# Early stage of an attention and gated-MLP kernel: VectorE takes all differences, one per head for q and k together, from operands in four blocks of columns

## The chip, the cores and the metric

The kernel runs on one core of a Trainium2 chip. Its engines work side by side, each through a queue of its own, in order: TensorE (PE in the profile) multiplies matrices, VectorE (DVE), ScalarE (ACT) and GpSimd (POOL) work element by element, and SyncE (SP) issues the DMAs. The metric is the time of one execution on the device in microseconds.

## The reference

Block-causal attention over 8 batches of 8 heads, 576 positions and a head size of 64, followed by a gated MLP over the 4608 tokens:

```python
scores = scale * q @ k.T                    # scale = 1/8
scores = where(block_i >= block_j, scores, -1e9)     # blocks of 64 positions
attn = exp(scores - max(scores)); attn = attn / (attn.sum() + 1e-9)
x = (attn @ v) with the heads side by side           # 4608 x 512
a = x @ w1; b = x @ w2                               # 512 x 1024 each
out = (a * b @ w3) @ w_out                           # 1024 x 1024, then 1024 x 512
```

## The kernel before

**Halves of a number.** Operands of the fast matmul form (fp32r) are kept as a high part, which is the number rounded by a cast, and a low part, the number minus the high part. A product then takes several passes. Every low part is thus a *difference*: a cast writes the high part, and a subtraction of two SBUF operands writes the low part. That subtraction is what the change is about.

**Pairs of heads.** Two heads share the 128 partitions: head j = 0 owns partitions 0 to 63, head j = 1 owns 64 to 127 (`own[j]`, the other half is `oth[j]`). There are 32 pairs, n = 0 to 31. The first four pairs, one batch, are called early (`EARLY = NPAIR`, that is 4). `load(n)` brings q, k and v of a pair into a tile `raw`, of which there are two.

**Scores in two passes.** For each head there are two tiles `hi[j]` and `lo[j]` of 128 x 2 x 576: block 0 belongs to q, block 1 to k. `s_tile` (L224) multiplies block 1 with block 0 of `hi[j]`, then of `lo[j]`, into one sum. In `hi[j]` the own half holds the high parts of q and k, the other half a copy of q's high part and k's low part. In `lo[j]` the own half holds q's low part and a copy of k's high part; the other half holds constants for the block mask and one row with the negated maximum of each query's block, which `shift` (L194) fills by DMA. `prep_qk` (L198) makes all of this in three steps: a cast of q and k together (L203, ScalarE for pairs 1 to 4, VectorE otherwise); two copies between tiles by DMA (L205, L206) and k's low part on GpSimd (L207); q's low part on GpSimd (L209). The two tiles per head have no second buffer.

**The mask's maxima.** `shift_mask` (L161) multiplies coarse bf16 copies of q and k block by block; VectorE reduces each product to its maximum (L183), joins two of the columns (L185), and PE transposes the result.

**The early stage.** Beside the attention of pairs 0 to 3 it prepares the weights: they arrive as 64-bit numbers, and `load_w` (L122) puts each chunk of 128 x 512 together with one instruction of ScalarE (L135) and four of VectorE (L136, L137, L138, L141). There are 40 chunks. 16 of them, of w1 and w2, go on through `load_split` (L145): a cast on ScalarE and a difference on GpSimd (L148). The rest feed the product of w3 and w_out (L360), whose own difference is VectorE's (L349). At the end of a pair `norm` (L321) divides by the sums (GpSimd for pairs 0 and 1, L325), and `finish_x` (L327) makes the high part of x on ScalarE and the low part on GpSimd (L335).

**The late stage.** From about 176 us PE alternates between the attention of pairs 4 to 31 and the MLP (`gen_moe`, L372) of batches already done. `pl` (L250, VectorE) and `gl` (L392, GpSimd) are differences there too, and GpSimd adds up the exponentials (L253).

**Order.** The order in which instructions are written comes from two strings per pair, `EARLY_PLAN` and `PLAN`: "B" takes the next step of `prep_qk` for the pair's second head, "A" for the next pair's first head, "M" the mask, "S" a score tile, "V" the product with v, "C" a step of the weights, "F" one of the MLP, "N", "R", "T" the end of a head or a pair, "Q" v and the next load. Each of the two plans has three "A" and three "B". A planner then places instructions on each engine by its own costs; the attention of early pairs goes ahead of the weights (`high_priority`); in the late stage the order on PE is the written one (`manual_schedule`).

Of the kernel before, what the change touches and what calls it, by code (L numbers as in the profile page):

```python
# [7 lines left out]
F32 = mybir.dt.float32  # L8
F32R = mybir.dt.float32r
# [49 lines left out]
def block_causal_attention__then__gated_mlp_kernel(ctx, tc, qkv, consts, ident_in, w1, w2, w3t, wout, out_t):  # L59
# [18 lines left out]

    hi = [cpool.tile([P, 2, S], F32R, name=f"hi{j}") for j in range(2)]
    lo = [cpool.tile([P, 2, S], F32R, name=f"lo{j}") for j in range(2)]
    w2h = cpool.tile([P, NC, DF], F32R, name="w2h")
    w2l = cpool.tile([P, NC, DF], F32R, name="w2l")

# [13 lines left out]
    cst = raws.tile([P, RAW], F32, tag="raw", name="cst")  # L99
    nc.sync.dma_start(out=cst[0:D, 0 : 2 * S], in_=consts)  # L100
    for j in range(2):
        nc.vector.tensor_copy(lo[j][oth[j]], cst[0:D, 0 : 2 * S].rearrange("p (t s) -> p t s", t=2))
    nc.gpsimd.memset(qd, 0.0)

    tl = {}
# [39 lines left out]
    def load_split(dst_h, dst_l, src):  # L145
        val = load_w(None, src.unsqueeze(1), 1)
        nc.scalar.copy(dst_h, val)
        nc.gpsimd.tensor_tensor(out=dst_l, in0=val, in1=dst_h, op=ALU.subtract)  # L148

    def load_rows(dst_h, dst_l, src, c):  # L150
        for h in range(2):
# [4 lines left out]
    def cast(n, dst, src, act):  # L156
        (nc.scalar.copy if 0 < n <= EARLY or act else nc.vector.tensor_copy)(dst, src)  # L157
# [3 lines left out]
    def shift_mask(n):  # L161
        r = raw_of[n]
        rqk = r[:, 0 : 2 * S].rearrange("p (t s) -> p t s", t=2)
        kb = work.tile([P, S], BF16, tag="kb", name=f"kb{n}")
        cast(n, kb, rqk[:, 1, :], CAST[1])
        for j in range(2):
            cast(n, qd[own[j], :, own[j]], rqk[own[j], 0, :].rearrange("p (i r) -> p i r", r=BLK), CAST[2])
        yield
        m = work.tile([P, 32], F32, tag="m", name=f"m{n}")

        groups = [((7, 0, 512),), ((8, 0, 512),), ((6, 0, 448), (0, 0, 64)), ((5, 0, 384), (1, 0, 128)),
                  ((4, 0, 320), (2, 0, 192)), ((3, 0, 256), (8, 512, 576))]
        for g, parts in enumerate(groups):
            t = ps_q.tile([P, 512], F32, tag="psq", name=f"mx{n}_{g}")
            at = 0
            done = []
            for i, a, b in parts:
                sc = t[:, at : at + b - a]
                nc.tensor.matmul(sc, qd[:, i, :], kb[:, a:b], start=True, stop=True)  # L179
                done.append((sc, 9 if a else i))  # L180
                at += b - a
            for sc, col in done:
                nc.vector.reduce_max(m[:, col : col + 1], sc, axis=AX.X)  # L183
            yield
        nc.vector.tensor_tensor(out=m[:, 8:9], in0=m[:, 8:9], in1=m[:, 9:10], op=ALU.max)  # L185
        mt = ps_q.tile([P, 512], F32, tag="psq", name=f"mt{n}")
        nc.tensor.transpose(out=mt[0:NB, 0:P], in_=m[:, 0:NB], identity=ident)
        ms = work.tile([16, P], F32R, tag="ms", name=f"ms{n}")
        nc.scalar.mul(out=ms[0:NB], in_=mt[0:NB, 0:P], mul=-1.0)
        ms_of[n] = ms  # L190
        shift(n, 0)
        yield

    def shift(n, j):  # L194
        row = lo[j][oth[j].start : oth[j].start + 1, 0, :].rearrange("p (i r) -> p i r", r=BLK)
        nc.sync.dma_start(out=row.bitcast(F32), in_=ms_of[n][0:NB, j * BLK : (j + 1) * BLK].bitcast(F32))

    def prep_qk(n, j):  # L198
        rqk = raw_of[n][:, 0 : 2 * S].rearrange("p (t s) -> p t s", t=2)
        o, x = own[j], oth[j]  # L200
        if j == 1:
            shift(n, 1)
        cast(n, hi[j][o], rqk[o], CAST[0])  # L203
        yield
        nc.sync.dma_start(out=hi[j][x, 0, :].bitcast(F32), in_=hi[j][o, 0, :].bitcast(F32))  # L205
        nc.sync.dma_start(out=lo[j][o, 1, :].bitcast(F32), in_=hi[j][o, 1, :].bitcast(F32))  # L206
        nc.gpsimd.tensor_tensor(out=hi[j][x, 1, :], in0=rqk[o, 1, :], in1=hi[j][o, 1, :], op=ALU.subtract)  # L207
        yield
        nc.gpsimd.tensor_tensor(out=lo[j][o, 0, :], in0=rqk[o, 0, :], in1=hi[j][o, 0, :], op=ALU.subtract)  # L209
        yield  # L210

    def prep_v(n, j):
# [11 lines left out]
    def s_tile(n, j, parts, p_early):  # L224
# [3 lines left out]
        for c, q0, q1, e0 in parts:  # L228
            kr = slice(c * P, min((c + 1) * P, S))
            ks = slice(0, kr.stop - kr.start)  # L230
            for s, src in enumerate((hi[j], lo[j])):
                nc.tensor.matmul(t[ks, at : at + q1 - q0], src[:, 1, kr], src[:, 0, q0:q1], start=(s == 0), stop=(s == 1))  # L232
            todo.append((c, ks, at + e0 - q0, e0, q1))
            at += q1 - q0
        for c, ks, at, q0, q1 in todo:
# [85 lines left out]
    def norm(n, x32, rr):  # L321
        nc.vector.reciprocal(rr, rr)
        rb = work.tile([P, S], F32, tag="tr", name=f"rb{n}")
        nc.vector.transpose(rb, rr.unsqueeze(2).broadcast_to([P, S // 32, 32]))
        (nc.gpsimd if n < 2 else nc.vector).tensor_tensor(out=x32, in0=x32, in1=rb, op=ALU.mult)  # L325

    def finish_x(n, x32):  # L327
        for h in range(2):
# [3 lines left out]
            xl = pool.tile([P, HALF], F32R, tag="xl", name=f"xl{n}_{h}", bufs=bufs)  # L332
            src = x32[:, h * HALF : (h + 1) * HALF]
            nc.scalar.copy(xh, src)
            nc.gpsimd.tensor_tensor(out=xl, in0=src, in1=xh, op=ALU.subtract)  # L335
            x_of[n // NPAIR, n % NPAIR, h] = (xh, xl)

    def gen_w(wp):
# [200 lines left out]
```

## Time and profile before

| | |
|---|---|
| median of 3 runs | 1026.23 us (1025.86 to 1026.67) |
| profiled execution, its own time | 1025.84 us |
| span of its instructions | 1024.1 us |
| mean granted TensorE clock | 0.98 |
| VectorE busy, whole span | 754.3 us (74%) |
| GpSimd busy, whole span | 599.1 us (58%) |

The page names an instruction group by line, engine, operation and tiles, output first: `hi<-raw,hi` writes `hi` from `raw` and `hi`. Behind the count stand the busy time in us, the mean duration of one in ns, the idle time of the engine ahead of these instructions and what ended it. A row of the stages gives the window, its length, the busy us of each engine with counts, then the granted clock of PE, the share of the DMA engines and GB/s.

### The profile page before, as it was taken

What the parts mean: (1) busy time and instruction counts of PE and PEld (TensorE: products, weight loads), DVE (VectorE), ACT (ScalarE), POOL (GpSimd) and SP (SyncE); (2) the same over time, 40 slices, a digit from 0 to 9 for tenths busy, and PEclk for the clock granted to TensorE, in tenths of its full rate; (3) what the DMA queues carried; (4) which work ended last, traced back from release to release, by engine and by line L of the source; (5) the groups of instructions that cost most, each with busy time, mean ns of one, the idle gap of its engine ahead of it and who ended that gap; (6) DMA issues with size and microseconds to landing.
All of it is one profiled execution on the core that took longest, in us unless ns stands there. A gap on an engine that the chain in (4) does not pass through costs nothing.

```text
span 1024.1 us, 18507 instructions
## 1 busy us (share of the span) xinstructions
PE 966.5 (94%) x6624; PEld 886.8 (87%) x6624; DVE 754.3 (74%) x1320; ACT 547.3 (53%) x1433; POOL 599.1 (58%) x625
## 2 busy tenths in 40 slices
PE   4789686999999999999999999999999999999998
PEld 2435344999999999999999999999999999999998
DVE  6999996787778777778777877777777777775100
ACT  4545455655565555556555556555555556554221
POOL 3334365766666676757575767666676757673211
PEclk9899898999999999999999999999999999999999
DMA  7765542221222222222222212221222221110000
GB/s 230 227 212 158 191 128 60 61 69 44 67 72 66 66 66 78 60 83 59 74 60 84 56 49 62 71 73 54 79 60 83 60 84 49 48 25 25 1 25 24
DMA packets 37437, 80.42 MB, mean 79 GB/s; under 512 B 5409, under 2 KB 21921, under 8 KB 37345
## 3 DMA queue, kind: packets, MB, share of 16 engines
q1 hardware_dynamic: 37344, 79.24, 25.7%
q8 instruction: 52, 0.85, 0.4%
q14 instruction: 41, 0.33, 0.1%
HBM read 50.76 MB, written 9.44 MB: 59 GB/s over the span
## 4 chain that ended last, share of the span: by engine, by line
PE 69%; DVE 18%; ACT 6%; issue 4%; DMA 1%; POOL 1%; DVEq 0%; SPq 0%; ACTq 0%; POOLq 0%
PE ab L383 29%; PE o L399 20%; PE s L232 7%; PE x L287 6%; DVE pl L250 5%; PE mx L179 3%; DVE wbits L138 2%; DVE wbits L136 2%; ACT p L247 2%; ACT ph L248 2%; DVE g L390 1%; PE w L360 1%; DVE m L183 1%; DVE wbits L137 1%; PE x L271 1%
## 5 line engine op out<-in xcount | busy, mean ns | idle before, releaser
L253 POOL TENSOR_TENSOR rsum<-rsum,p 128x448 f32<-128x448 f32 x224 | 175.9, 785 | 107.1 <-ACT p L247 100.5
L250 DVE TENSOR_TENSOR pl<-p,ph 128x448 fp32r<-128x448 f32 x168 | 148.9, 900 | 60.7 <-ACT ph L248 59.9
L392 POOL TENSOR_TENSOR gl<-g,gh 128x288 fp32r<-128x288 f32 x128 | 107.5, 840 | 120.4 <-ACT gh L391 119.0
L391 ACT CAST gh<-g 128x288 fp32r<-128x288 f32 x128 | 55.5, 433 | 217.1 <-DVE g L390 217.1
L383 PE MATMUL ab<-xh,w2h 128*128 128x288 f32 x512 | 153.6, 300 | 0.0
L399 PE MATMUL o<-gh,wh 128*128 128x288 f32 x512 | 153.4, 300 | 0.0
L383 PE MATMUL ab<-xl,w1h 128*128 128x288 f32 x512 | 151.0, 295 | 1.3 <-POOL xl L335 1.3
L383 PE MATMUL ab<-xh,w1h 128*128 128x288 f32 x512 | 151.1, 295 | 0.0
L383 PE MATMUL ab<-xl,w2h 128*128 128x288 f32 x512 | 150.9, 295 | 0.0
L383 PE MATMUL ab<-xh,w1l 128*128 128x288 f32 x512 | 150.9, 295 | 0.0
L399 PE MATMUL o<-gl,wh 128*128 128x288 f32 x512 | 150.8, 295 | 0.0
L399 PE MATMUL o<-gh,wl 128*128 128x288 f32 x512 | 150.8, 295 | 0.0
L383 PE MATMUL ab<-xh,w2l 128*128 128x288 f32 x512 | 150.8, 295 | 0.0
L183 DVE TENSOR_REDUCE m<-mx 128x1 f32<-128x512 f32 (+6 forms) x320 | 128.8, 449 | 23.8 <-PE mx L179 22.0
L248 ACT ACTIVATE ph<-s 128x288 fp32r<-128x288 f32 x336 | 131.5, 393 | 0.0
L232 PE MATMUL s<-hi 128*128 128x288 f32 (+4 forms) x384 | 123.8, 334 | 6.3 <-ACT pe L240 4.8
L207 POOL TENSOR_TENSOR hi<-raw,hi 64x576 fp32r<-64x576 f32 x64 | 92.5, 1446 | 37.1 <-ACT hi L157 25.1
L247 ACT ACTIVATE p<-s 128x448 f32<-128x448 f32 x224 | 85.5, 381 | 44.9 <-PE s L232 44.9
L250 DVE TENSOR_TENSOR pl<-rsum,ph 128x288 fp32r<-128x288 f32 x112 | 74.8, 687 | 46.4 <-ACT ph L248 46.3
L390 DVE TENSOR_TENSOR g<-ab,a 128x288 f32<-128x288 f32 x128 | 57.7, 451 | 69.6 <-PE ab L383 61.3
L232 PE MATMUL s<-lo 128*128 128x288 f32 (+4 forms) x384 | 106.4, 306 | 2.1 <-DMA lo<-ms 2.1
L209 POOL TENSOR_TENSOR lo<-raw,hi 64x576 fp32r<-64x576 f32 x64 | 95.6, 1494 | 19.7 <-ACT hi L157 15.0
(73 smaller groups left out, 2449.1 us busy)
## 6 DMA issues: line engine op xcount, KB each, us to landing
raw<-in_qkv SPq DMA_DIRECT2D x32, 896.0 KB
hi<-hi SPq DMA_DIRECT2D x64, 144.0 KB
lo<-hi SPq DMA_DIRECT2D x64, 144.0 KB
out_t<-o SPq DMA_DIRECT2D x64, 144.0 KB
wraw<-in_w3t SPq DMA_DIRECT2D x16, 512.0 KB
wraw<-in_w SPq DMA_DIRECT2D x16, 512.0 KB
wraw<-in_wout SPq DMA_DIRECT2D x8, 512.0 KB
lo<-ms SPq DMA_DIRECT2D x64, 2.2 KB
```

Of the source, the lines that this page charges most:

```text
L183: nc.vector.reduce_max(m[:, col : col + 1], sc, axis=AX.X)
L207: nc.gpsimd.tensor_tensor(out=hi[j][x, 1, :], in0=rqk[o, 1, :], in1=hi[j][o, 1, :], op=ALU.subtract)
L209: nc.gpsimd.tensor_tensor(out=lo[j][o, 0, :], in0=rqk[o, 0, :], in1=hi[j][o, 0, :], op=ALU.subtract)
L232: nc.tensor.matmul(t[ks, at : at + q1 - q0], src[:, 1, kr], src[:, 0, q0:q1], start=(s == 0), stop=(s == 1))
L247: nc.scalar.activation(p32, t[ks, at : at + w], AF.Exp, scale=SCALE)
L248: nc.scalar.activation(ph[ks, o : o + w], t[ks, at : at + w], AF.Exp, scale=SCALE)
L250: nc.vector.tensor_tensor(out=low, in0=p32, in1=ph[ks, o : o + w], op=ALU.subtract)
L253: nc.gpsimd.tensor_tensor(out=r, in0=r, in1=p32, op=ALU.add)
L383: nc.tensor.matmul(t[:, 0:HALF], l[:, c, fs], r, start=(c == 0 and s == 0), stop=(c == NC - 1 and s == 2))
L390: nc.vector.tensor_tensor(out=g32, in0=acc[1][:, 0:HALF], in1=a32, op=ALU.mult)
L392: nc.gpsimd.tensor_tensor(out=gl[:, f, :], in0=g32, in1=gh[:, f, :], op=ALU.subtract)
L399: nc.tensor.matmul(t[:, 0:HALF], l[:, f, es], r[:, f, :], start=(f == 0 and s == 0), stop=(f == NF - 1 and s == 2))
```

## The change

- One tile `qk[j]` of 128 x 4 x 576 takes the place of `hi[j]` and `lo[j]`. Blocks 0 and 1 are q's for the two passes, blocks 2 and 3 are k's. In the own half the cast writes blocks 0 and 3 (`0::3`), the high parts of q and k; one subtraction writes blocks 1 and 2 (`1:3`), the low parts. One DMA copies the high parts to blocks 0 and 2 of the other half (`0::2`), whose blocks 1 and 3 hold the constants. The first pass now multiplies q's high part with k's low part (own half) and with k's high part (other half), the second q's low part with k's high part and the mask.
- `prep_qk` has two steps in place of three. Its one subtraction is VectorE's for pairs 0 to 4, GpSimd's later.
- The differences of the weights, of early x, and the product in `norm` for pairs 0 and 1 move from GpSimd to VectorE.
- The maximum of two columns becomes a reduction over two columns, for all pairs.

```diff
-    hi = [cpool.tile([P, 2, S], F32R, name=f"hi{j}") for j in range(2)]
-    lo = [cpool.tile([P, 2, S], F32R, name=f"lo{j}") for j in range(2)]
+    qk = [cpool.tile([P, 4, S], F32R, name=f"qk{j}") for j in range(2)]
...
-        nc.vector.tensor_copy(lo[j][oth[j]], cst[0:D, 0 : 2 * S].rearrange("p (t s) -> p t s", t=2))
+        nc.vector.tensor_copy(qk[j][oth[j], 1::2, :], cst[0:D, 0 : 2 * S].rearrange("p (t s) -> p t s", t=2))
...
         nc.scalar.copy(dst_h, val)
-        nc.gpsimd.tensor_tensor(out=dst_l, in0=val, in1=dst_h, op=ALU.subtract)
+        nc.vector.tensor_tensor(out=dst_l, in0=val, in1=dst_h, op=ALU.subtract)
...
-        nc.vector.tensor_tensor(out=m[:, 8:9], in0=m[:, 8:9], in1=m[:, 9:10], op=ALU.max)
+        nc.vector.reduce_max(m[:, 8:9], m[:, 8:10], axis=AX.X)
...
-        row = lo[j][oth[j].start : oth[j].start + 1, 0, :].rearrange("p (i r) -> p i r", r=BLK)
+        row = qk[j][oth[j].start : oth[j].start + 1, 1, :].rearrange("p (i r) -> p i r", r=BLK)
...
-        cast(n, hi[j][o], rqk[o], CAST[0])
+        high, low = qk[j][o, 0::3, :], qk[j][o, 1:3, :]
+        cast(n, high, rqk[o], CAST[0])
         yield
-        nc.sync.dma_start(out=hi[j][x, 0, :].bitcast(F32), in_=hi[j][o, 0, :].bitcast(F32))
-        nc.sync.dma_start(out=lo[j][o, 1, :].bitcast(F32), in_=hi[j][o, 1, :].bitcast(F32))
-        nc.gpsimd.tensor_tensor(out=hi[j][x, 1, :], in0=rqk[o, 1, :], in1=hi[j][o, 1, :], op=ALU.subtract)
-        yield
-        nc.gpsimd.tensor_tensor(out=lo[j][o, 0, :], in0=rqk[o, 0, :], in1=hi[j][o, 0, :], op=ALU.subtract)
+        nc.sync.dma_start(out=qk[j][x, 0::2, :].bitcast(F32), in_=high.bitcast(F32))
+        (nc.vector if n <= EARLY else nc.gpsimd).tensor_tensor(out=low, in0=rqk[o], in1=high, op=ALU.subtract)
         yield
...
-            for s, src in enumerate((hi[j], lo[j])):
-                nc.tensor.matmul(t[ks, at : at + q1 - q0], src[:, 1, kr], src[:, 0, q0:q1], start=(s == 0), stop=(s == 1))
+            for s in range(2):
+                nc.tensor.matmul(t[ks, at : at + q1 - q0], qk[j][:, 2 + s, kr], qk[j][:, s, q0:q1], start=(s == 0), stop=(s == 1))
...
-        (nc.gpsimd if n < 2 else nc.vector).tensor_tensor(out=x32, in0=x32, in1=rb, op=ALU.mult)
+        nc.vector.tensor_tensor(out=x32, in0=x32, in1=rb, op=ALU.mult)
...
-            nc.gpsimd.tensor_tensor(out=xl, in0=src, in1=xh, op=ALU.subtract)
+            (nc.vector if n < EARLY else nc.gpsimd).tensor_tensor(out=xl, in0=src, in1=xh, op=ALU.subtract)
```

## The prediction

> **What bounds the kernel now.** I read the page first, then the busy time by stage, then VectorE's waits in the early stage, then its groups of instructions with shapes kept apart, and last the order of time on VectorE and GpSimd side by side.
>
> ```profile
> span 1024.1 us, 18507 instructions
> PE 966.5 (94%) x6624; PEld 886.8 (87%) x6624; DVE 754.3 (74%) x1320; ACT 547.3 (53%) x1433; POOL 599.1 (58%) x625
> ...
> DVE  6999996787778777778777877777777777775100
> ```
>
> Over the whole span PE is the busy one. The third row, VectorE in 40 slices of 25.6 us, shows that this average mixes two programs: for the second to the sixth slice VectorE is at nine tenths or more. The stages apart (us, then busy time of PE, PEld, DVE, ACT, POOL with counts):
>
> ```profile
> 10.00:60.00 50.00, 33.95 (x105) 19.02 (x106) 44.47 (x84) 24.74 (x49) 14.93 (x11) 0.88 0.67 217
> 60.00:110.00 50.00, 46.53 (x138) 23.45 (x136) 47.40 (x81) 24.28 (x47) 20.53 (x12) 0.95 0.62 189
> 110.00:161.00 51.00, 33.30 (x106) 17.50 (x104) 49.26 (x74) 25.52 (x50) 26.50 (x18) 0.83 0.45 142
> 161.00:176.00 15.00, 11.62 (x49) 8.45 (x49) 7.80 (x18) 9.71 (x22) 7.33 (x7) 0.79 0.13 25
> ...
> 200.00:900.00 700.00, 695.37 (x5152) 675.46 (x5151) 543.50 (x960) 405.21 (x1116) 468.41 (x507) 1.00 0.23 67
> ```
>
> From 10 to 161 us VectorE is busy 44.47 + 47.40 + 49.26 = 141.1 of 151 us, PE 113.8. From 200 us PE has 695.4 of 700, and only 4.6 us could be won there. So the early stage hangs on VectorE, the late one on PE, and 161 to 176 is the passage. What VectorE waited for up to 161 us (total, times, longest):
>
> ```profile
> DVE hi L157 <- DMA raw<-in_qkv: 5.8, 1, 5.8
> DVE m L183 <- PE mx L179: 4.9, 3, 1.9
> DVE wbits L136 <- ACT wbits L135: 2.8, 4, 1.3
> ```
>
> The first is the start. The other two add 7.7 us: the queue of VectorE hardly ever runs dry. Now what fills it (count, then busy us and mean ns of one), and with it the least, median and longest duration of three of these lines:
>
> ```profile
> L138 DVE SCALAR_TENSOR_TENSOR wbits<-wraw,wbits 128x512 int32<-128x512 int32 x40 | 34.6, 867 | 0.4
> L136 DVE TENSOR_SCALAR wbits<-wbits 128x512 f32<-128x512 f32 x40 | 25.2, 633 | 3.0 <-ACT wbits L135 2.8
> L137 DVE TENSOR_SCALAR wbits<-wbits 128x512 int32<-128x512 int32 x40 | 22.6, 569 | 0.3
> L141 DVE SCALAR_TENSOR_TENSOR wbits<-wraw,wbits 128x512 int32<-128x512 int32 x16 | 16.1, 1007 | 0.1
> L141 DVE SCALAR_TENSOR_TENSOR w<-wraw,wbits 128x512 int32<-128x512 int32 x16 | 13.0, 812 | 0.1
> ...
> L141 DVE SCALAR_TENSOR_TENSOR wo<-wraw,wbits 128x512 int32<-128x512 int32 x8 | 6.7, 831 | 0.1
> L349 DVE TENSOR_TENSOR wl<-w,wh 128x512 fp32r<-128x512 f32 x8 | 5.5, 683 | 0.0
> ...
> L102 DVE CAST lo<-cst 64x1152 fp32r<-64x1152 f32 x2 | 3.3, 1653 | 0.4 <-DMA cst<-in_consts 0.4
> ...
> L157 DVE CAST hi<-raw 64x1152 fp32r<-64x1152 f32 x2 | 1.5, 754 | 5.8 <-DMA raw<-in_qkv 5.8
> ...
> L325 DVE TENSOR_TENSOR x<-x,rb 128x576 f32<-128x576 f32 x1 | 0.7, 746 | 0.0
> ...
> L138 DVE SCALAR_TENSOR_TENSOR wbits<-wraw,wbits x40: 639/688/1886, 15.6 to 156.3; 128x512 int32<-128x512 int32 x40
> ...
> L136 DVE TENSOR_SCALAR wbits<-wbits x40: 410/420/1632, 12.2 to 151.9; 128x512 f32<-128x512 f32 x40
> ...
> L137 DVE TENSOR_SCALAR wbits<-wbits x40: 370/421/1503, 15.1 to 155.1; 128x512 int32<-128x512 int32 x40
> ```
>
> One shape, one operation, and yet 688 ns at the median and 1886 at the longest. The order of time says when (start, us, engine):
>
> ```profile
> 72.84 0.68 DVE L138 SCALAR_TENSOR_TENSOR wbits<-wraw,wbits 128x512 int32<-128x512 int32 x1
> 73.05 1.61 POOL L148 TENSOR_TENSOR w1l<-wbits,w1h 128x512 fp32r<-128x512 f32 x1 [1.35 <-ACT w1h L147]
> 73.44 1.50 DVE L137 TENSOR_SCALAR wbits<-wbits 128x512 int32<-128x512 int32 x1
> ...
> 91.11 0.68 DVE L349 TENSOR_TENSOR wl<-w,wh 128x512 fp32r<-128x512 f32 x1
> 91.71 0.68 DVE L138 SCALAR_TENSOR_TENSOR wbits<-wraw,wbits 128x512 int32<-128x512 int32 x1
> ```
>
> L137 takes 1.50 instead of 0.42 us while GpSimd subtracts beside it, and ends 0.28 us after GpSimd: 73.44 + 1.50 against 73.05 + 1.61. So a GpSimd subtraction isn't free beside VectorE here; VectorE pays for a good part of it by standing still. The last two rows show that an undisturbed 0.68 us costs only 0.60 from start to start, 0.08 less than its record.
>
> **What goes: the standing still.** Mean minus median, times the count: L138 40 x (867 - 688) = 7.2 us; L136 40 x (633 - 420) = 8.5; L137 40 x (569 - 421) = 5.9. For L141 the undisturbed time is that of L138, as 91.71 shows for the same operation: 16 x (1007 - 688) = 5.1, 16 x (812 - 688) = 2.0, 8 x (831 - 688) = 1.1. The two constant copies L102 against the same shape in L157: 2 x (1653 - 754) = 1.8. Together 31.6 us. After the change GpSimd has no subtraction left before the passage, so I take all of it as gone; the lower bound is nothing, were the stretch of another cause.
>
> **What comes: the subtractions themselves on VectorE.** Two undisturbed subtractions fix the price: 683 ns for 512 columns and 746 for 576, 0.98 ns a column.
> - Weights (load_split), 8 of w1 and 8 of w2: as L349, 683 - 80 = 0.60 us each, 9.6 us.
> - q and k together, one per head on 64x1152 in place of two on GpSimd. GpSimd's rows count them up to 161 us:
>
> ```profile
> L209 POOL TENSOR_TENSOR lo<-raw,hi 64x576 fp32r<-64x576 f32 x9 | 17.2, 1910 | 15.5 <-ACT hi L157 15.0
> L207 POOL TENSOR_TENSOR hi<-raw,hi 64x576 fp32r<-64x576 f32 x9 | 14.2, 1576 | 25.5 <-ACT hi L157 17.6 <-DVE hi L157 4.3 <-issue 3.2
> ```
>
> Nine heads; the tenth falls into the passage. No row has the new form, with blocks 0 and 3 on one side and 1 and 2 on the other. Nearest: 746 + 576 x 0.98 = 1.31, less 0.08 = 1.23 us. Bounds: 0.75 (the cast of the same 64x1152, L157) and 2 x 0.746 = 1.49. Nine times: 11.1 us (6.8 to 13.4).
> - The lower halves of x (finish_x), six up to 161 us at 683 - 224 x 0.98 = 0.46, less 0.08: 2.3 us. The two products in norm, 0.746 - 0.08 each: 1.3 us.
> - The maximum in shift_mask becomes a reduction of two columns, one instruction for one: taken at nothing; even at the 0.68 us of a 512-column one, five would be 3.4.
>
> Together 24.3 us. VectorE's queue gets shorter by 31.6 - 24.3 = 7.3 us, to some 134 of 151, and stays the longest; behind it lies PE with 113.8. I count this as won in full, because the next work stands ready there.
>
> The Trainium skill has a rule against the overlap used here, in "VectorE: DVE Perf Modes", section "Two Vector instructions with no wait between them": an instruction whose start quadrant differs from the one before it starts only when all earlier ones have ended. The second head's subtraction starts at partition 64. By this rule it and its successor would each lose the 0.08 us, 4 x 2 x 0.08 = 0.6 us, and the sum would be that much smaller; no row here separates it out.
>
> **New waits.** VectorE's queue is in order. On GpSimd each subtraction could wait for ScalarE's cast at nobody's cost; now what is queued behind it (weight chunks, the mask's reductions that PE waits for) stands too. The casts:
>
> ```profile
> L157 ACT CAST hi<-raw 64x1152 fp32r<-64x1152 f32 x7 | 8.0, 1147 | 0.7 <-issue 0.7
> ...
> L147 ACT CAST w2h<-wbits 128x512 fp32r<-128x512 f32 x8 | 5.0, 619 | 11.2 <-DVE wbits L141 11.2
> ```
>
> 33 instructions are concerned (16 + 9 + 6 + 2). Upper bound, a whole cast each time: 24 x 0.62 + 9 x 1.15 = 25.2 us; lower bound nothing. I take the nearest row, VectorE behind ScalarE at L136: 2.8 us in 40 instructions, 0.07 each, so 2.3 us: as there, other chunks can be put between. L349 waits in the same way and shows 0.0.
>
> **The passage.** PE stood before the last lower half of x:
>
> ```profile
> 174.52 1.77 POOL L335 TENSOR_TENSOR xl<-x,xh 128x288 fp32r<-128x288 f32 x2
> ...
> 175.36 0.40 PE L383 MATMUL ab<-xl,w1h 128*128 128x288 f32 x1 [1.32 <-POOL xl L335]
> ```
>
> GpSimd got to it behind two subtractions of q and k and two of v. On VectorE it no longer queues there: 1.3 us less at best; the tenth q/k subtraction can put 1.2 us ahead of it. I take 1.0 less (1.3 less to 0.5 more).
>
> **Copies and the late stage.** Two copies of 144 KB per head become one of 288 KB: the same bytes, one issue less on SP, and the one now carries k as well to the other half. In the late stage GpSimd keeps the subtraction, one in place of two:
>
> ```profile
> L207 POOL TENSOR_TENSOR hi<-raw,hi 64x576 fp32r<-64x576 f32 x51 | 72.7, 1425 | 3.8
> ...
> PE x L287 <- DVE pl L250: 3.8, 13, 0.3
> ```
>
> It costs GpSimd at most 2 x 1.43 us, as now, and GpSimd is busy 468 of 700. PE waits there for a slow subtraction of VectorE only 3.8 us in all. Taken at nothing; bounds 4 less and, if all 51 met the longest wait of 0.3, 15 more.
>
> **Sum.** -7.3 + 2.3 - 1.0 + 0 = -6.0 us. The profiled execution took 1025.84 us (span 1024.1), so 1019.8; the median of the runs shown, 1026.23, lies 0.4 above it: 1020.2, rounded 1020.
>
> **Rivals.**
> 1. *No change.* Not VectorE's throughput but the chain through each pair (scores, mask, exponentials, product) sets the early end, and the time won becomes idle time. For it, PE's waits up to 161 us:
>
> ```profile
> PE mx L179 <- DVE m L183: 23.2, 10, 6.4
> ```
>
> PE does wait, for reductions queued behind weights. But it waits for VectorE, which itself waited 7.7 us: against it. Time: 1026.2 - 1.0 = 1025.
> 2. *Slower: VectorE stops at the subtractions.* Place: prep_qk and load_split, behind ScalarE's casts. It decides from 8.3 / 33 = 0.25 us of wait per instruction. At half a cast each, 12.6 us instead of 2.3: 1020.2 + 10.3 = 1030.5. For it: the cast now has the consumer on an engine without slack. Against it: 0.07 and 0.0 in the rows for L136 and L349.
> 3. *The spread views tie the copy to the subtraction.* The copy reads blocks 0 and 3, the subtraction writes 1 and 2 between them; if the planner takes the views by their outer bounds, the subtraction waits for the copy's landing, and the kernel doesn't do what it says. The price of a landing from issue to the matmul that needs it:
>
> ```profile
> 17.50 0.87 SPq L196 DMA_DIRECT2D lo<-ms  x1
> ...
> 20.89 0.83 PE L232 MATMUL s<-lo 128*128 128x288 f32 x2
> ```
>
> 3.4 us, nine times 30.6 us; half hidden by other chunks: 1020.2 + 15.3 = 1035.5. No row speaks for or against.
> 4. *The longer GpSimd instruction in the late stage.* VectorE stands up to 1.4 us longer behind one subtraction of 2.9 us than behind 1.43. If one in four of 51 reaches PE: 18 us, 1038. Against it: PE's 3.8 us above. The Trainium skill, "SBUF — State Buffer", section "Who interferes with whom", has the rule for this: who issues first holds the pair of ports that VectorE and GpSimd share for the whole instruction, and the other fully blocks. The rows at 73.05 agree.
>
> **How the numbers follow.** Forecast 0.58, alone 1013 (no new waits, nine subtractions at 0.75, the passage at its best) to 1024 (nine at 1.49, the passage at its worst); rival 1 0.15; rival 2 0.18; rival 3 0.06; rival 4 0.03. About 0.2%, 2 us, is what a measurement of this kernel can tell from no change. Faster: the forecast and the part of rival 1 in which a little is won, 0.60. Same: the rest of rival 1 and rival 2 with waits near 0.25 us, 0.18. Slower: 0.22. The range of 1012 to 1031 takes in the forecast, rival 1 and rival 2 up to half a cast, and leaves out rivals 3 and 4 and the worst of 2.
>
> **What would show it.** L138 near 688 ns in the mean, L136 and L137 near 420; no GpSimd subtraction before the passage; the new 64x1152 at about 1.3 us; the last L138 (now at 156.3) some 5 us earlier; the stage from 200 us as long as before. Wrong, if L138 stays near 867 with GpSimd idle, if a wait of VectorE for ScalarE's hi or w1h grows beyond 8 us in all, or if PE's busy time per 700 us in the late stage falls.

## The result, and the profile after

The changed kernel takes 1007.94 us (median of 4 runs, 1006.22 to 1008.37), against 1026.05 us (4 runs, 1025.73 to 1026.67): a ratio of 0.9819, with a 95% interval of 0.9807 to 0.9831. The prediction was 1020 us, in a range from 1012 to 1031. The direction was right; the gain is 18.1 us where 6.0 were forecast, and the time lies below the range.

The page of the changed kernel, its profiled execution (1008.37 us), with the rows that were shown of before and GpSimd's below VectorE's:

```profile
span 1006.6 us, 18165 instructions
PE 961.6 (96%) x6594; PEld 886.1 (88%) x6624; DVE 718.8 (71%) x1356; ACT 547.9 (54%) x1433; POOL 521.1 (52%) x525
...
DVE  7999997767777777777777767777777777774100
...
POOL 0000006667665766666666657576666766573211
```

GpSimd does nothing in the second to the sixth slice, VectorE is as full as before. The stages (window, length, busy us of PE, PEld, DVE, ACT, POOL with counts, clock, DMA share, GB/s):

```profile
10.00:60.00 50.00, 36.78 (x112) 20.30 (x114) 48.67 (x104) 27.50 (x53) 0.00 (x0) 0.90 0.79 250
60.00:110.00 50.00, 48.95 (x159) 25.10 (x160) 48.73 (x100) 29.26 (x58) 0.00 (x0) 1.00 0.66 204
...
200.00:900.00 700.00, 695.55 (x5126) 675.13 (x5150) 518.21 (x966) 403.85 (x1113) 461.14 (x455) 1.00 0.23 65
```

The late stage stands as it stood: 695.55 of 700 us of PE against 695.37. All of the gain is early, and there VectorE is busy 48.7 of every 50 us, where it was 44.5 and 47.4.

So the early stage is split into what VectorE does and what it waits for. The window runs from 7.7 us, by when VectorE's first two casts are over, to the end of the last lower half of pair 3's x, which is where the early stage hands over: 176.3 us before, 154.3 after. First before, then after:

```profile
7.70:176.30 168.60, 126.79 (x396) 68.96 (x397) 151.44 (x253) 86.06 (x173) 71.81 (x48) 0.88 0.54 168
```

```profile
7.70:154.30 146.60, 117.89 (x388) 65.35 (x391) 141.65 (x287) 85.68 (x168) 2.52 (x2) 0.91 0.63 193
```

The window is 22.0 us shorter. VectorE is busy 151.44 against 141.65, 9.8 less; it isn't busy for 168.60 - 151.44 = 17.2 against 146.60 - 141.65 = 5.0 us, 12.2 less. What follows the window takes 1024.1 - 176.3 = 847.8 before and 1006.6 - 154.3 = 852.3 after, 4.5 more. -9.8 - 12.2 + 4.5 = -17.5, the difference of the spans. More than half of the gain in the window is waiting that has gone, and the prediction had no such term.

VectorE's waits in that window (total, times, longest), before:

```profile
DVE m L183 <- PE mx L179: 7.5, 4, 2.6
DVE tr L311 <- PE x L271: 3.5, 3, 2.2
DVE wbits L136 <- ACT wbits L135: 2.8, 4, 1.3
DVE pl L250 <- ACT ph L248: 1.6, 1, 1.6
```

and after:

```profile
DVE xl L333 <- ACT xh L332: 0.8, 1, 0.8
DVE wl L347 <- ACT wh L346: 0.8, 1, 0.8
DVE m L183 <- PE s L230: 0.7, 1, 0.7
DVE qk L207 <- ACT qk L157: 0.7, 1, 0.7
DVE wbits L136 <- ACT wbits L135: 0.3, 1, 0.3
DVE m L183 <- PE mx L179: 0.2, 1, 0.2
```

VectorE used to stop for PE, at the maxima and at the sums' transposes, for 7.5 + 3.5 = 11.0 us; 0.7 + 0.2 of that are left. And its groups after, up to 145 us (count, busy us, mean ns of one, idle time before):

```profile
L138 DVE SCALAR_TENSOR_TENSOR wbits<-wraw,wbits 128x512 int32<-128x512 int32 x39 | 26.7, 683 | 0.1
L136 DVE TENSOR_SCALAR wbits<-wbits 128x512 f32<-128x512 f32 x40 | 16.5, 417 | 0.3 <-ACT wbits L135 0.3
L137 DVE TENSOR_SCALAR wbits<-wbits 128x512 int32<-128x512 int32 x39 | 16.3, 418 | 0.0
L207 DVE TENSOR_TENSOR qk<-raw,qk 64x1152 fp32r<-64x1152 f32 x9 | 12.1, 1342 | 0.8 <-ACT qk L157 0.7
L141 DVE SCALAR_TENSOR_TENSOR w<-wraw,wbits 128x512 int32<-128x512 int32 x16 | 10.9, 680 | 0.0
L141 DVE SCALAR_TENSOR_TENSOR wbits<-wraw,wbits 128x512 int32<-128x512 int32 x15 | 10.3, 686 | 0.1
...
L141 DVE SCALAR_TENSOR_TENSOR wo<-wraw,wbits 128x512 int32<-128x512 int32 x8 | 5.5, 685 | 0.0
L148 DVE TENSOR_TENSOR w1l<-wbits,w1h 128x512 fp32r<-128x512 f32 x8 | 5.5, 684 | 0.1
...
L333 DVE TENSOR_TENSOR xl<-x,xh 128x288 fp32r<-128x288 f32 x6 | 2.5, 454 | 0.0
...
L323 DVE TENSOR_TENSOR x<-x,rb 128x576 f32<-128x576 f32 x3 | 2.2, 749 | 0.0
...
L102 DVE CAST qk<-cst 64x1152 fp32r<-64x1152 f32 x2 | 1.5, 754 | 0.0
```

The means are now what the medians were: 683 for 867, 417 for 633, 418 for 569 ns.

### The profile page after: what moved, and what is told of

Read it like the earlier page. It is cut to its first block, busy times and chain, and to the rows that moved or that the text cites. A ratio compares the mean times of both kernels' runs of the same rounds, so it can differ in the third digit from the quotient of the medians.

```text
span 1006.6 us, 18165 instructions
## 1 busy us (share of the span) xinstructions
PE 961.6 (96%) x6594; PEld 886.1 (88%) x6624; DVE 718.8 (71%) x1356; ACT 547.9 (54%) x1433; POOL 521.1 (52%) x525
## 4 chain that ended last, share of the span: by engine, by line
PE 60%; DVE 23%; ACT 9%; issue 6%; DMA 2%; DVEq 0%; ACTq 0%
PE ab L381 23%; PE o L397 20%; DVE pl L248 7%; PE s L230 6%; PE x L285 4%; PE mx L179 3%; DVE g L388 2%; ACT ph L246 2%; PE w L358 2%; ACT p L245 2%; DVE m L183 2%; DVE wbits L138 1%; DVE x L323 1%; DVE rb L322 1%; DVE qk L157 1%
## 5 line engine op out<-in xcount | busy, mean ns | idle before, releaser
L251 POOL TENSOR_TENSOR rsum<-rsum,p 128x448 f32<-128x448 f32 x224 | 178.3, 796 | 120.4 <-ACT p L245 113.6
L230 PE MATMUL s<-qk 128*128 128x288 f32 (+4 forms) x768 | 160.7, 317 | 9.2 <-DMA qk<-ms 3.5
L381 PE MATMUL ab<-xh,w2l 128*128 128x288 f32 x512 | 151.4, 296 | 0.0
L207 POOL TENSOR_TENSOR qk<-raw,qk 64x1152 fp32r<-64x1152 f32 x54 | 144.3, 2672 | 2.0
L220 POOL TENSOR_TENSOR vs<-raw,vs 128x320 fp32r<-128x320 f32 x56 | 49.9, 891 | 174.2 <-ACT vs L157 174.2
L230 PEld LDWEIGHTS s<-qk 128*128 128x128 f32 (+1 forms) x768 | 116.9, 184 | 26.1 <-issue 6.1
L183 DVE TENSOR_REDUCE m<-mx 128x1 f32<-128x512 f32 (+6 forms) x320 | 128.6, 449 | 15.8 <-PE mx L179 13.2
L246 ACT ACTIVATE ph<-s 128x288 fp32r<-128x288 f32 x336 | 131.3, 392 | 0.0
L285 PE MATMUL x<-ph,vs 128*128 128x128 f32 x336 | 104.1, 319 | 0.0
```

The costliest lines, as they stand in the source:

```text
L207: (nc.vector if n <= EARLY else nc.gpsimd).tensor_tensor(out=low, in0=rqk[o], in1=high, op=ALU.subtract)
L230: nc.tensor.matmul(t[ks, at : at + q1 - q0], qk[j][:, 2 + s, kr], qk[j][:, s, q0:q1], start=(s == 0), stop=(s == 1))
L246: nc.scalar.activation(ph[ks, o : o + w], t[ks, at : at + w], AF.Exp, scale=SCALE)
L251: nc.gpsimd.tensor_tensor(out=r, in0=r, in1=p32, op=ALU.add)
L285: nc.tensor.matmul(xps[:, to : to + w], v[:, c, :], pr[:, a : a + w], start=(u < 2 and s == 0), stop=(u in (0, len(PV) - 1) and s == len(p ...
L381: nc.tensor.matmul(t[:, 0:HALF], l[:, c, fs], r, start=(c == 0 and s == 0), stop=(c == NC - 1 and s == 2))
```

## The experiments

### Is it the standing still?

Two kernels keep the changed kernel and put GpSimd subtractions beside it again, whose results nobody reads. In these two the order of instructions on VectorE, PE and ScalarE is the changed kernel's own. The first has dummies for 14 of the 16 weight chunks, the heads of pairs 0 to 3 and the x of pairs 0 to 2; a memset at the start fills their constant operand:

```diff
+    def beside(src, rows, w):
+        nc.gpsimd.tensor_tensor(out=w2l[rows, 3, 0:w], in0=src.bitcast(F32), in1=w2h[rows, 3, 0:w].bitcast(F32), op=ALU.subtract)
...
+            beside(dst_h, slice(0, P), 512)
...
+            beside(high[:, 0, :], o, S)
+            beside(high[:, 1, :], o, S)
...
+                beside(xh, slice(0, P), HALF)
```

> The changed kernel, with GpSimd made to subtract again beside it in the early stage: behind each difference of weights, of q and k (pairs 0 to 3) and of x (pairs 0 to 2) GpSimd subtracts a constant from the same high part, in the old shapes, into columns of w2l that nobody has filled yet. Nobody uses these results, and the order on VectorE, ScalarE and PE is that of the changed kernel, instruction for instruction; only 4 of the 16 weights have no such partner at the end of w2 (2 chunks). Theory 1 (standing still behind GpSimd was the cost): L138 goes back from 683 ns to some 850 ns in the mean, the early stage gets 20 to 30 us longer, 1028 to 1038 us. Theory 2 (the gain is the shorter way from q and k to the scores and the order that follows from it): within 5 us of the changed kernel, 1008 to 1013 us.

Measured: 1037.72 us (ratio to before 1.0104, 1.0075 to 1.0133), 29.8 us more than the changed kernel. Its window up to the last lower half:

```profile
7.70:183.90 176.20, 124.45 (x388) 68.72 (x390) 168.03 (x287) 85.52 (x168) 69.54 (x38) 0.86 0.50 160
```

and one of its groups, the line that was L138:

```profile
L142 DVE SCALAR_TENSOR_TENSOR wbits<-wraw,wbits 128x512 int32<-128x512 int32 x40 | 31.3, 781 | 0.1
```

The same 287 instructions of VectorE are busy 168.03 instead of 141.65 us: 26.4 us of standing still (683 to 781 ns in the line shown, where some 850 was expected), brought about by 69.54 - 2.52 = 67.0 us of work on another engine alone. The waits grow by only 3.2 (8.2 against 5.0). The mechanism of the prediction is shown, and near the size that it gave, 31.6.

The second has one dummy of 64x1152 per head, for the eight heads of pairs 0 to 3:

```diff
+        if n < EARLY:
+            nc.gpsimd.tensor_tensor(out=w2l[o, 2:4, 0:S], in0=w2h[o, 2:4, 0:S].bitcast(F32), in1=high, op=ALU.subtract)
```

> The changed kernel; behind each difference of q and k of pairs 0 to 3 GpSimd subtracts beside it in the same shape (64x1152) into columns that nobody uses. Order on VectorE, ScalarE and PE as in the changed kernel, instruction for instruction. Standing still alone: of the 29.8 us that 68 us of such work cost, the share of some 21 us, 9 us: 1015 to 1020 us, VectorE's waits for PE below 3 us.

Measured: 1018.58 us (0.9931, 0.991 to 0.9951), 10.6 us over the changed kernel. Its window:

```profile
7.70:164.32 156.62, 118.20 (x391) 65.08 (x389) 153.83 (x287) 84.96 (x168) 34.66 (x10) 0.91 0.56 179
```

The same 287 instructions of VectorE are busy 12.2 us longer than in the changed kernel. Eight dummies cost about what the eight real subtractions on VectorE cost (8 x 1.34 = 10.7).

The other way round: the kernel before without any subtraction in the early stage. GpSimd fills the low parts with zeros instead, so the differences of q, k, w1, w2 and early x are left out and VectorE gets nothing for them:

```diff
-        nc.gpsimd.tensor_tensor(out=dst_l, in0=val, in1=dst_h, op=ALU.subtract)
+        nc.gpsimd.memset(dst_l.bitcast(F32), 0.0)
...
+        if n <= EARLY:
+            nc.gpsimd.memset(hi[j][x, 1, :].bitcast(F32), 0.0)
...
+            if n < EARLY:
+                nc.gpsimd.memset(xl.bitcast(F32), 0.0)
```

> The kernel before, with all early differences on GpSimd (weights, q and k of pairs 0 to 4, x of pairs 0 to 3) left out and zeros written in their place by GpSimd memsets, which read nothing. VectorE does no additional work; the two products in norm stay on GpSimd. Theory 1 (standing still, and VectorE's throughput sets the end): the 30 us of standing still go and nothing comes for it: 996 to 1003 us. If something else, such as PE or the chain through the pairs, sets the end once VectorE is freed: 1005 to 1010 us, about the changed kernel.

Measured: 1001.40 us (0.9755, 0.9739 to 0.9772), 24.7 us less than before. The zeros for x are written at the start, so its window ends with the last high part of pair 3's x, at 149.3 us. This window, and two of its groups:

```profile
7.70:149.30 141.60, 115.99 (x385) 62.74 (x384) 128.25 (x253) 83.78 (x166) 22.51 (x37) 0.96 0.62 198
```

```profile
L138 DVE SCALAR_TENSOR_TENSOR wbits<-wraw,wbits 128x512 int32<-128x512 int32 x40 | 27.1, 682 | 0.4
...
L157 DVE CAST hi<-raw 64x1152 fp32r<-64x1152 f32 x2 | 10.5, 5245 | 5.3 <-DMA raw<-in_qkv 5.2
```

VectorE's window has 23.2 us less of busy time and 141.60 - 128.25 = 13.4 us of waiting, 3.8 less than before. Two things follow. Taking the standing still away takes less than a quarter of the waits away; it comes out of the time nearly in full. And from here to the changed kernel the time grows by only 6.5 us, though VectorE takes on all the subtractions, 24 us by the prediction's count: 13.4 us more of busy time in the window (not all 24, because the two casts of the last row stood for 9.0 us here and do not in the changed kernel), 8.4 less of waiting, and 1.7 more behind it (999.9 - 149.3 = 850.6, against 852.3).

The layout of the tiles alone, with the subtractions left on GpSimd:

```diff
-        nc.gpsimd.tensor_tensor(out=hi[j][x, 1, :], in0=rqk[o, 1, :], in1=hi[j][o, 1, :], op=ALU.subtract)
-        yield
-        nc.gpsimd.tensor_tensor(out=lo[j][o, 0, :], in0=rqk[o, 0, :], in1=hi[j][o, 0, :], op=ALU.subtract)
+        nc.gpsimd.tensor_tensor(out=low, in0=rqk[o], in1=high, op=ALU.subtract)
```

> The new tiles alone: every early difference and the two products in norm stay on GpSimd, q and k in one instruction per head, one copy, two steps, and the reduction for the maximum. Theory 1 (standing still behind GpSimd is the cost, the tiles do nothing): GpSimd's early work is as long as before, 1024 to 1028 us. Theory 3 (the tiles, with the order that the planner makes of them, took VectorE's waits for PE away, which fell from 11 to 1 us): 1014 to 1019 us.

Measured: 1027.34 us (1.0014, 1.0003 to 1.0025), no gain, and at most 0.25% of loss.

### Which part brings how much?

The changed kernel with the old two tiles, two VectorE subtractions per head:

> The old tiles hi and lo with their two copies and three steps, but all early differences on VectorE: two of 64x576 per head in place of one of 64x1152. Theory 1 (standing still): two of 0.75 us in place of one of 1.34 us, nine times 0.16 = 1.5 us more work: 1009 to 1011 us. Theory 3 (the tiles make the gain: one copy, one subtraction, one step less): most of the gain is missing, 1016 to 1022 us.

Measured: 1008.94 us (0.9836, 0.9821 to 0.985), 1.0 more than the changed kernel (1.7 by the two ratios). With the run before this one: the blocks of columns and the one instruction in place of two are worth 1 to 2 us at most.

The changed kernel with the maximum of two columns as it was:

> The changed kernel with the maximum of two columns again as one operation on two operands of one column. In the late stage it should stand still behind GpSimd again, 0.7 to 1.1 us in place of 0.15, 28 times. If nothing there waits for VectorE, no difference: 1007 to 1009 us. If the mask's chain is on PE's path: up to 20 us more.

Measured: 1007.37 us (0.9818, 0.9801 to 0.9835), no difference.

Of the moved subtractions, only those of q and k on VectorE (weights, x and norm back on GpSimd); only those of the 16 weight chunks (all else as before); and all but those of q and k:

> The changed kernel with weights, x and norm back on GpSimd; only q and k are VectorE's in the early stage, in the new tiles. Theory 1 (standing still): 53% of it comes back, 17 us, and 13 us of work leave VectorE: 3 to 4 us slower than the changed kernel, 1011 to 1012 us. Theory 2 (shorter way from q and k to the scores): as fast as the changed kernel, 1007 to 1009 us.

> The kernel before with the 16 differences of the weights alone on VectorE. 25.5 of 66.4 us of early GpSimd subtraction go. By the sum of standing still less added work alone: 12 us go, 9.6 us come, 1023 to 1024 us. If VectorE's waits go in proportion as well, as in the whole change: 38% of 18 us, 1018 to 1020 us.

> The changed kernel, but the one difference of q and k per head stays on GpSimd in the early stage too; weights, x and norm are VectorE's. Theory 1 (standing still): of 66.4 us of early GpSimd subtraction before the change 31.4 come back, 47%, so some 15 us of 31.6 us standing still, and 12 us of work leave VectorE: 3 us slower than the changed kernel, 1011 us. Theory 2 (shorter way from q and k to the scores): most of the gain is lost, 1020 to 1025 us.

Measured: 1012.85 us (0.9872, 0.9857 to 0.9886) for q and k alone; 1011.76 (0.9861, 0.9846 to 0.9876) for the weights alone; 1015.57 (0.9896, 0.988 to 0.9913) without q and k. The first lies within 1 us of the first theory. The second is far better than any theory had it; the third lies between two. The two parts alone gain 13.0 and 14.3 us, together 27.3, where the whole change gains 18. So they share something that can be had only once. Their windows, q and k first:

```profile
7.70:161.70 154.00, 120.16 (x387) 67.05 (x389) 143.55 (x262) 85.84 (x170) 36.73 (x28) 0.90 0.59 187
```

```profile
7.70:159.40 151.70, 119.83 (x392) 65.72 (x393) 144.84 (x268) 86.08 (x172) 51.98 (x32) 0.93 0.58 186
```

Waiting is down from 17.2 to 10.5 us with q and k, to 6.9 with the weights, to 5.0 with both. Either part takes 6.7 or 10.3 us from the same store, both together 12.2. In spans the two parts gain 27.5 us and the whole 17.5; of the 10.0 between them 4.8 are this waiting, and 4.7 are busy time of VectorE, which falls by 7.9 and 6.6 us with either part and by 9.8 with both.

### What is this store?

Three explanations of the lost waits were tried. First, that it hangs on where pair 3 stands among the weights; here the rest of the weights is written ahead of pair 3, which loses its priority over them:

```diff
-                with tc.high_priority(offset=0) if early else nullcontext():
+                with tc.high_priority(offset=0) if n < EARLY - 1 else nullcontext():
...
+        if n == NPAIR - 1:
+            fill(weights, 100)
```

> The changed kernel with all remaining weights written ahead of pair 3, and pair 3 without its priority: both transposes of its attention come behind the last weight chunk on VectorE, as in the kernel before, while pairs 0 to 2 keep their places. Theory A (the passage got shorter because pair 3 is already through when the weights end): the passage is as long as before, 12 us or so behind the last weight, and the kernel takes 1014 to 1020 us. Theory B (the passage got shorter because its steps no longer queue on GpSimd or stand still): no more than 3 us slower than the changed kernel, 1008 to 1011 us.

Measured: 1009.72 us (0.9846, 0.983 to 0.9863), 1.8 more than the changed kernel. The place of pair 3 doesn't matter much.

Second, that the scores had waited for GpSimd's slow differences of q and k, and PE for the scores. In the kernel with one dummy per head, the dummy now writes the real low parts a second time, so that the scores wait for GpSimd:

> The changed kernel; for pairs 0 to 3 GpSimd computes the difference of q and k a second time, over the one of VectorE, so that the scores wait for GpSimd; the planner's order shifts a little with it. If GpSimd's place on the way to the scores was what made VectorE wait for PE (11 us before, 1 us after): those waits are 5 us or more again and it is 4 to 8 us slower than with the same work beside. If only the standing still counts: within 2 us of that kernel.

Measured: 1027.94 us (1.0015, 1.0004 to 1.0027), 9.4 over that kernel, with VectorE's waiting at 10.7 us in place of 2.8 (the planner's order differs a little between the two). It shows that such a delay would hurt. It doesn't show that the kernel before had it: there the waits of the scores for GpSimd are not among PE's, while here a row `PE s L233 <- POOL qk L210: 4.1, 2, 3.7` has appeared. And in the kernel whose low parts were zeros, where nothing but memsets of 0.57 us stood on GpSimd between q, k and the scores, 13.4 us of waiting were left.

Third, that the waits are slack: VectorE arrives early at results of PE, and work put in between uses the time. Then useless work in the kernel before must be cheaper than its length. Dummy subtractions on VectorE, for the heads of pairs 0 to 3, for 12 of the weight chunks and for the x of pairs 0 to 2; all real ones stay on GpSimd:

```diff
+    def more(out, src, other):
+        nc.vector.tensor_tensor(out=out, in0=src, in1=other.bitcast(F32), op=ALU.subtract)
...
+            more(w2l[:, 3, 0:512], dst_h, w2h[:, 3, 0:512])
...
+            more(w2l[o, 2:4, 0:S], hi[j][o, :, :], w2h[o, 2:4, 0:S])
...
+                more(w2l[:, 3, 0:HALF], xh, w2h[:, 3, 0:HALF])
```

> The kernel before, with work added to VectorE that nobody waits for: it subtracts a constant from the same high parts, beside 12 of the 16 weights, the q and k of pairs 0 to 3 and the x of pairs 0 to 2, in the shapes of the change; GpSimd keeps its differences. Added: 12 x 0.60 + 8 x 1.23 + 6 x 0.38 = 19.3 us. Theory 4 (VectorE's early waits are slack that added work fills, so that work moved there costs less than its sum): VectorE's 17 us without work fall to 3 to 9 and the time rises by 5 to 11 us, 1031 to 1037 us. Theory 5 (the waits stay as they are, and fell in the change for another reason): the whole 19 us come on top, 1043 to 1048 us.

Measured: 1038.23 us (1.0116, 1.01 to 1.0133), 11.9 more than before and 1.2 above the range of the theory that it was to test, well below that of the other. Its window, and VectorE's waits in it:

```profile
7.70:188.00 180.30, 125.11 (x395) 68.82 (x396) 175.46 (x279) 86.55 (x173) 73.03 (x48) 0.88 0.49 156
```

```profile
DVE pl L258 <- ACT ph L256: 1.9, 1, 1.9
DVE m L189 <- PE mx L185: 1.1, 2, 0.8
DVE wbits L140 <- ACT wbits L139: 0.2, 1, 0.2
```

VectorE is busy 24.0 us longer (175.46 against 151.44), and its waiting falls from 17.2 to 180.30 - 175.46 = 4.8, by 12.3: the same fall as with the change, in a kernel where every difference is still GpSimd's. Half of the added work was free. So the waits go where VectorE has more to do, though the differences stay on GpSimd. The planner's order isn't held fixed in it: with the dummies it places VectorE's other instructions differently, from 12 us on.

With the dummies of the weights alone:

> The kernel before with only the 12 weight instructions of that work added to VectorE, 7.2 us. Theory 4: most of it disappears in the waits, 1025 to 1029 us. Theory 5: 1032 to 1034 us.

Measured: 1031.37 us (1.0052, 1.0035 to 1.0069), 5.0 more, between the two theories; VectorE is busy 8.5 us longer (159.95) and waits 4.8 us less (12.3). 4.8 of 8.5 is a little over half, 12.3 of 24.0 is half. VectorE up to the handover, from the traces of these kernels (us):

| kernel | busy | waiting |
|---|---|---|
| nothing added to VectorE: before | 151.4 | 17.2 |
| the same, new tiles alone | 150.6 | 18.6 |
| the same, zeros in place of the differences | 128.3 | 13.4 |
| part added: dummies of the weights | 160.0 | 12.3 |
| the same, all differences but those of q and k | 146.7 | 12.7 |
| the same, q and k alone | 143.6 | 10.5 |
| the same, weights alone | 144.8 | 6.9 |
| all added: dummies for all | 175.5 | 4.8 |
| the same, changed kernel | 141.7 | 5.0 |
| the same, in the old tiles | 144.1 | 5.1 |
| the same, weights ahead of pair 3 | 142.7 | 6.8 |
| the same, GpSimd dummies beside | 168.0 | 8.2 |
| the same, one GpSimd dummy per head beside | 153.8 | 2.8 |
| the same, the scores waiting for GpSimd | 155.5 | 10.7 |

The changed kernel and the two with GpSimd dummies have the same order on VectorE; the others differ from it and from the kernel before. With nothing added VectorE waits 13 to 19 us, with all of it 3 to 8 unless a delay of the scores is put in; in between the amount of work alone doesn't settle it.

### A better version

PE stands for 6.8 us in the passage (below). To have the MLP's first steps come later there, `DELAY`, the number of its steps left out in pair 4, goes from 3 to 6 and to 9:

```diff
-DELAY = 3
+DELAY = 6
```

> The changed kernel with DELAY 6 in place of 3: in pair 4 the first six steps of the MLP are left to later, so that PE goes on with the attention of pair 4 where it now stands 6.8 us before the last high part of x and then runs at a granted clock of 0.55. If pair 4 is ready there: 1001 to 1005 us. If PE then stands before pair 4's exponentials and maxima instead: 1007 to 1010 us.

> The changed kernel with DELAY 9. If the order of DELAY 6 is a lucky one of two phases: back to 1004 to 1008 us. If every later start of the MLP helps: 996 to 999 us.

> The kernel before with DELAY 6. If the 8 us that DELAY 6 brought the changed kernel lie in the late stage's order on PE, which no longer meets unfinished subtractions for the product with v, they come here as well: 1018 to 1020 us. If they need the earlier end of pair 3: 1025 to 1027 us.

Measured: 1000.16 us with 6 (0.9748, 0.9733 to 0.9762), 1002.29 with 9 (0.977, 0.9755 to 0.9786), and 1020.31 in the kernel before with 6 (0.9949, 0.9931 to 0.9966). The first is the fastest version of all, 7.8 us better than the changed kernel and better than either of its two forecasts; the second lies between its two. The reason isn't the one it was tried for: PE still stands in the passage, `PE s L230 <- ACT ph L246: 10.2, 1, 10.2`. PE from 170 to 900 us, first of the changed kernel, then with 6:

```profile
170.00:900.00 730.00, 725.26 (x5346) 703.91 (x5371) 541.47 (x1011) 420.64 (x1160) 481.95 (x476) 1.00 0.23 65
```

```profile
170.00:900.00 730.00, 730.00 (x5430) 711.51 (x5430) 546.13 (x1020) 425.05 (x1173) 507.07 (x484) 1.00 0.22 65
```

PE's last 4.7 us of waiting in the late stage are gone, among them its 13 waits for VectorE's `pl` (3.8 us); the other 3.1 us were not traced. The likely reason, not tested by itself, is that a step of the attention now has another step of the MLP beside it. It works in the kernel before too (-5.4), where the same waits go, so it is a matter of the late order and not of the change.

## Why the prediction was wrong, point by point

**Standing still, -31.6: right in kind, a little small.** The six lines of the weight chunks took, mean times count, 118.5 us (34.7 + 25.3 + 22.8 + 16.1 + 13.0 + 6.6) and take 88.1 with the same 40, 16, 16 and 8 (27.3 + 16.7 + 16.7 + 10.9 + 11.0 + 5.5): -30.4 where -29.8 was counted. The constant copies fell from 1653 to 754 ns, -1.8 as counted. Successive records overlap a little, though, and less where an instruction stands. Without the overlap the six lines fell by 32.5 us, and L312, which wasn't counted, by 1.5.

**Added work, +24.3: right for each instruction, short in number.** Weights 684, q and k 1342 where 1.31 us was worked out, x 454 where 0.46, norm 749 ns. By the records 16 x 0.68 + 9 x 1.34 + 6 x 0.45 + 2 x 0.75 = 27.1; less the 0.08 for each of 33, 24.5 us. The layout in four blocks costs the subtraction next to nothing. But ten heads and eight lower halves come ahead of the handover, not nine and six: without the overlap, what moved takes 27.7 us there. Two subtractions of pair 4 (1.7 us) lie ahead of it before and not after. Together: -32.5 - 1.8 - 1.5 + 27.7 - 1.7 = -9.8, as measured, where the prediction had -7.3. Both of its terms were 3 to 4 us small, and that they nearly cancel is luck.

The rule on two VectorE instructions with no wait between them was weighed there at 0.6 us. By the written order the first subtraction of q and k in these rows is that of pair 3's second head, which starts at partition 64, and the other that of pair 4's first head, at partition 0. VectorE after, from 127 to 133 us (start, us):

```profile
127.73 0.69 DVE L138 SCALAR_TENSOR_TENSOR wbits<-wraw,wbits 128x512 int32<-128x512 int32 x1
128.45 1.35 DVE L207 TENSOR_TENSOR qk<-raw,qk 64x1152 fp32r<-64x1152 f32 x1
129.84 0.69 DVE L141 SCALAR_TENSOR_TENSOR wbits<-wraw,wbits 128x512 int32<-128x512 int32 x1
130.56 0.78 DVE L309 STREAM_TRANSPOSE tr<-x 64x576 f32<-64x576 f32 x1
131.28 1.31 DVE L207 TENSOR_TENSOR qk<-raw,qk 64x1152 fp32r<-64x1152 f32 x1
132.51 0.67 DVE L148 TENSOR_TENSOR w2l<-wbits,w2h 128x512 fp32r<-128x512 f32 x1
```

The subtraction at 128.45 starts 0.03 us after its predecessor's end (127.73 + 0.69 = 128.42), and its successor 0.04 after its own (129.80); the one at 131.28 starts 0.06 ahead of its predecessor's end (131.34), and its successor 0.08 ahead of its own (132.59). The Trainium skill, "VectorE: DVE Perf Modes", section "Two Vector instructions with no wait between them", has it that an instruction with another start quadrant than the last waits until all earlier ones have finished. The rows agree: some 0.1 us on each side of the one, four or five times, under 1 us in all.

**The step that failed: the waits.** The prediction read VectorE's 7.7 us of waits as proof that the queue hardly runs dry, let them stand, and put 2.3 us of new ones on top. Of the passage, where VectorE was busy 7.80 of 15 us, it counted only 1.0. It thereby charged the whole 24.3 us of added work, as though each microsecond of it lengthened the stage. In fact VectorE had 17.2 us of waiting ahead of the handover, and 12.2 of it went when the work was added. Against the +1.3 of the prediction (2.3 - 1.0) that is a miss of 13.5 us; with 2.5 more from the queue and 4.5 the other way behind the handover it makes up the 11.5 us by which the span missed. The dummies in the kernel before take away the same 12.3 with every difference still on GpSimd, and the zeros, with nothing added, only 3.8. The new waits themselves were sized well: behind ScalarE the moved subtractions wait 0.8 (x) + 0.7 (q and k) = 1.5 us.

PE's waits for the maxima, `PE mx L179 <- DVE m L183`, fell as well, from 23.2 us to 1.4, but that is another matter. In the kernel before with all dummies on VectorE they stay, up to the handover, while VectorE's own waits go:

```profile
PE mx L185 <- DVE m L189: 20.2, 10, 7.9
```

With one GpSimd dummy per head beside the changed kernel they are 10.2 us, while VectorE waits 2.8. So a wait of PE for VectorE didn't mean that VectorE waited too, and rival 1, which was set aside by weighing the two against each other, couldn't be judged from them; it fell because the time won in VectorE's queue did come out of the stage.

**The passage and the late stage, -1.0 and 0: the wrong sign.** 4.5 us are given back behind the handover at 154.3 us. PE's longest wait ends just ahead of it, at 153.5, and a low clock lies on both sides:

```profile
PE ab L381 <- ACT xh L332: 6.8, 1, 6.8
```

```profile
145.00:150.00 5.00, 1.68 (x8) 1.33 (x6) 4.84 (x10) 1.47 (x3) 0.00 (x0) 0.50 0.00 0
150.00:155.00 5.00, 1.50 (x4) 1.21 (x5) 3.93 (x6) 3.08 (x10) 2.52 (x2) 0.50 0.16 22
155.00:160.00 5.00, 5.00 (x24) 4.87 (x23) 3.23 (x5) 2.43 (x7) 2.27 (x2) 0.56 0.39 163
```

PE has nothing left to do until pair 3's x is there, and after the wait it runs at 0.50 to 0.56 of full clock until 160 us. The first 25.7 us behind the handover, before and after, in both of which PE is busy throughout:

```profile
176.30:202.00 25.70, 25.70 (x196) 25.03 (x195) 20.83 (x39) 15.43 (x43) 18.99 (x21) 1.00 0.24 73
```

```profile
154.30:180.00 25.70, 25.70 (x176) 24.81 (x176) 19.32 (x39) 14.87 (x41) 17.24 (x16) 0.90 0.21 59
```

By the two clocks, an estimate, 25.7 x 0.10 = 2.6 of the 4.5 us lie there. The rest is open, and no run took the wait or the low clock away by itself.

**Rivals.** 1 (no change): no, as said above. 2 (VectorE stops at the subtractions): no, its threshold was 0.25 us for each of 33, and 1.5 us in all came. 3 (copy and subtraction tied together): no; a late pair's copy is issued at 161.58 and its subtraction starts at 162.37, 0.8 us later, when GpSimd's queue gets there, where a landing was 3.4. 4 (longer GpSimd instruction): it is longer, 2672 ns in the mean, but from 200 to 900 us PE waits for VectorE's subtraction 3.5 us in 12 places, against 3.8 in 13 before.

**The signs named.** L138 at 683, L136 and L137 at 417 and 418, no GpSimd subtraction before the passage, 1.34 us for the new form, the late stage unchanged: all came. The last L138 was to be "some 5 us" earlier and is 9.4 earlier (146.9 for 156.3): the one sign that spoke of the time, and it showed the miss.

**Left open.** Why the weights alone empty the store so far (10.3 us by 9.6 us of work), and why it stays at 12.7 us when only q and k are left on GpSimd: the order in which the planner places the work differs between these kernels, and that was not separated from the amount of work. A delay of the scores by GpSimd fills the store too (10.7 us for 2.8), so in the second of them it may have a part.

## What to carry to other kernels

When work is moved onto the engine that sets a stage, split the stage into that engine's busy time and its waits first: the waits are slack that part of the added work may go into (here half of it), so that charging all of it gives an upper bound. A subtraction on GpSimd beside a busy VectorE isn't free: here 67 us of it cost 26 us of standing still, about as much as VectorE needs to do the work itself (27.7). A term is tested best by putting the suspected cost alone back into the faster kernel, as dummies that leave the order of all else as it is.

## What the runs showed of the hardware

A GpSimd subtraction can be the one that stands, and for long. Before, with VectorE's queue full of instructions of 0.68 us that kept their time, one took more than twice as long as the next of the same size:

```profile
91.72 4.15 POOL L209 TENSOR_TENSOR lo<-raw,hi 64x576 fp32r<-64x576 f32 x1 [3.29 <-ACT hi L157]
95.93 1.76 POOL L207 TENSOR_TENSOR hi<-raw,hi 64x576 fp32r<-64x576 f32 x1
```

And GpSimd's memsets, which read nothing, left VectorE's two-input instructions alone (L138 at 682 ns in that kernel) but held the cast of 64x1152, one input, for 5245 ns in the mean in place of 754. The Trainium skill, "SBUF — State Buffer", section "Who interferes with whom", says that a VectorE instruction with two SBUF inputs contends with a GpSimd instruction that reads and not with one that only writes, and that one in a 2-port mode contends with GpSimd. L138 agrees; the cast agrees if it runs in such a mode, which no row says. Either way, "no subtraction on GpSimd" is not the same as "nothing on GpSimd".
